# A fold without a product, one question at the end, and a start in another order: four small edits to an attention and experts kernel

## The chip, the cores and the metric

One core of a Trainium2 chip runs the kernel. The metric is device microseconds (us) of one execution; lower is better. The engines are TensorE (PE in the profile, its weight loads PEld), VectorE (DVE), ScalarE (ACT), GpSimd (POOL) and SyncE (SP), which issues most transfers. Each takes its own list of instructions in order and waits on semaphores for the others.

## The reference

Attention in which a query sees only the keys of its own cluster, and behind it a layer of experts in which each row goes to one expert of eight:

```python
# q, k, v: (4, 8, 768, 64); centroids: (8, 16, 64)
q_assign = argmax(normalized(q) @ normalized(centroids).T)   # 16 clusters per head; k_assign likewise
mask = q_assign[..., :, None] == k_assign[..., None, :]
scores = where(mask, q @ k.T / sqrt(64), -1e9)
x = softmax(scores) @ v            # heads side by side: (3072, 512)
logits = x @ w_gate                # 8 experts
e = argmax(logits);  gate = softmax(logits)[e]
y[rows of e] = relu(x[rows of e] @ w1[e]) @ w2[e]      # w1: 512 x 1024, w2: 1024 x 512
out = gate[:, None] * y
```

## The kernel before

Two heads make a pair, and there are 16 pairs (4 batches, 4 pairs each). The attention part is a list of jobs at numbered steps. A step makes three scores (`score`), then its jobs of part 0, then the three products with v of the step before (`attend`), then its jobs of part 1. For a pair, `turn` transposes q and k, `similar` and `similar2` make the similarities with the centroids and turn them, `assign` and `assign2` find the one-hots of the clusters, and `put` transposes those into `ohT`, which the scores add as a mask.

The start, before the first score:

```python
make_identity(nc, ident)
nc.vector.tensor_copy(ident_b, ident)
...   # norms of the centroids: three ScalarE functions, then seven VectorE steps
cps = ps_m.tile([P, 512], F32, name="mps")
nc.tensor.transpose(cps[:, 0:P], cn.rearrange("p a d -> p (a d)"), ident)
...
def turn(g, piece):
    ps = ps_s.tile([P, 2, 512], F32, name="sps").rearrange("p a c -> p (a c)")
    for i in range(4 if piece else 8):
        nc.tensor.transpose(ps[:, i * P : (i + 1) * P], ...q or k of the pair..., ident)
    flat = qk[g].rearrange("p w s -> p (w s)")
    if piece == 0:
        nc.vector.tensor_scalar_mul(flat[:, 0:S], ps[:, 0:S], D**-0.5)
        nc.scalar.copy(flat[:, S:1024], ps[:, S:1024])
    else:
        nc.scalar.copy(flat[:, 1024 : 2 * S], ps[:, 0 : 2 * S - 1024])
...
for g in range(NG):
    n = g * TG                      # TG = 4 steps for a pair
    if g == 1:
        for f, a in ((turn, (g, 0)), (turn, (g, 1)), (similar, (g,)), (similar2, (g,))):
            at(-1 if f is similar2 else -2, 1, f, *a)
    else:
        at(n - 4, 0, turn, g, 0)
        at(n - 4, 1, turn, g, 1)
        at(n - 3, 0, similar, g)
        at(n - 3, 1, similar2, g)
    at(n - 2, 0, assign, g)
    at(n - 2, 0, assign2, g)
    at(n - 1, 0, put, g)
```

The experts' part works in groups: eight experts, with two or three blocks of 128 rows and one last block of 32 rows each, and two groups of a single block of 128 for what overflows. (Three blocks have been worked ahead, during and behind attention.) For each group, `layer1` makes the hidden rows, the next group's rows are transposed, and `layer2` makes the sums. The 32 rows would use a quarter of PE's columns; so four products of two hidden blocks each stand side by side in the four quarters of an accumulator, and their four partial sums have to be added across quarters. Before, that was a product with `fold`, four 32x32 identities on top of each other:

```python
def wide():                                   # three of these, in turn
    return ps_s.tile([P, 2, 512], F32, name="sps")

def rows_out(g, j, m, zp):
    zo = p1.tile([P, Dm], F32, name="zo", bufs=3)
    nc.scalar.activation(zo[0:m], zp[0:m], AF.Copy, scale=...gate of the rows...)
    ins = nc.gpsimd.indirect_dma_start(out=out[:, :], ..., in_=zo[0:m], ...)     # scatter

def layer2(g):
    last = len(g["n"]) - 1
    zq = zc = None
    if g["n"][last] < P:
        zq = wide()
        n = FB * RQ // P                      # 2
        for i in range(n):
            for t in range(P // RQ):          # 4 quarters
                nc.tensor.matmul(zq[t * RQ : (t + 1) * RQ, 0, :],
                    lhsT=g["h"][:, t * n + i, last * P : last * P + RQ],
                    rhs=g["w"][1][:, t * n + i, :], start=(i == 0), stop=(i == n - 1))
        zc = p1.tile([P, Dm], F32, name="zo", bufs=3)
        nc.vector.tensor_copy(zc, zq[:, 0, :])
    for j, m in enumerate(g["n"]):
        if m < P:
            continue
        zp = wide()[:, 0, :]
        for fb in range(FB):                  # 8
            nc.tensor.matmul(zp, lhsT=g["h"][:, fb, j * P : (j + 1) * P], rhs=g["w"][1][:, fb, :], ...)
        rows_out(g, j, P, zp)
    if zc is not None:
        zf = wide()[0:RQ, 0, :]
        nc.tensor.matmul(zf, lhsT=fold, rhs=zc, start=True, stop=True)
        rows_out(g, last, RQ, zf)
```

At the end two numbers, found on the chip, are asked for by every engine: whether more overflow groups are needed than two, and whether the inputs call for a general path. Neither is so for these inputs, and both bodies are jumped over:

```python
nx = nc.values_load(xe[0:1, NX : NX + 1], min_val=0, max_val=NX)
general = nc.values_load(xe[0:1, NX + 1 : NX + 2], min_val=0, max_val=1)
with tc.If(nx > XU):
    ...   # more groups, in a loop
...
with tc.If(general > 0):
    in_general(...)
```

## Time and profile before

| | |
|---|---|
| time, median of 3 runs | 864.28 us (863.96 to 864.37) |
| span of the profiled execution | 862.4 us |
| PE busy | 832.5 us, 97% |
| DVE, ACT, POOL busy | 307.7, 271.2, 107.4 us |
| mean granted PE clock | 0.993 |

The page of the profile divides the span into 40 slices of 21.6 us. A digit is the busy share of an engine in a slice in tenths (9 is 90% or more), and in the row PEclk it is the granted clock of PE in tenths of full speed. A line of a group or of the timeline has the source line (L345), the engine, the operation, what is written and read, the form of the tiles and a count; an fp32 product shows as two records. In square brackets stands how long the engine had been idle and what ended the wait. The chain of waits follows the work that ended last back to the start, and "issue" in it is time for which the profile shows no cause. Sequencer steps (register loads, branches, semaphores, drains) aren't counted as busy; the trace keeps a record of each.

Attention takes the first 430 us or so, the experts the rest.

### The profile page before, as it was taken

Reading aid. Unit: us, or ns where it says so; the run is one execution under the profiler, and the core shown is the slowest. Engines: PE = TensorE matmul, PEld = TensorE weight load, DVE = VectorE, ACT = ScalarE, POOL = GpSimd, SP = SyncE. Lnnn points to the kernel's source line nnn. Section 1 sums busy time; section 2 is a strip of 40 time slices with the busy share of each in tenths; the row PEclk is TensorE's granted clock in tenths of the full one; section 3 lists DMA queues with packets and bytes.
Section 4 is the critical chain, followed back from the end, with each engine's and each line's share of the span. In section 5 each row is a group of like instructions: output and inputs, shape, how many; then the busy total and the mean of one; then the engine's idle time right before and its main releaser. Section 6 shows DMA issues by size and latency. Waiting matters only on the chain.

```text
span 862.4 us, 10765 instructions
## 1 busy us (share of the span) xinstructions
PE 832.5 (97%) x4397; PEld 435.3 (50%) x4397; DVE 307.7 (36%) x543; ACT 271.2 (31%) x422; POOL 107.4 (12%) x165
## 2 busy tenths in 40 slices
PE   4999999999999999999999999999999999999994
PEld 3444544444445444444576646645444454545472
DVE  2655566565565665875543101010101010101000
ACT  3554544554545555544311111111111111110010
POOL 3000000000000000130004211302020303010010
PEclk8999999999999999999999999999999999999998
DMA  9025320482222122210060245434242423312010
GB/s 203 1 57 217 88 55 11 121 251 56 55 81 59 46 55 56 93 38 1 8 274 15 66 141 205 159 110 152 110 150 110 164 98 119 136 67 90 24 38 7
DMA packets 76186, 81.69 MB, mean 95 GB/s; under 512 B 52831, under 2 KB 56927, under 8 KB 75616
## 3 DMA queue, kind: packets, MB, share of 16 engines
q1 hardware_dynamic: 70208, 60.82, 23.0%
q0 software_dynamic: 5248, 20.04, 6.5%
q8 instruction: 37, 0.61, 0.3%
q14 instruction: 21, 0.17, 0.1%
q10 hardware_dynamic: 672, 0.05, 0.1%
HBM read 68.26 MB, written 13.68 MB: 95 GB/s over the span
## 4 chain that ended last, share of the span: by engine, by line
PE 46%; issue 38%; POOL 8%; DVE 5%; ACT 1%; DMA 0%; POOLq 0%; ACTq 0%; DVEq 0%
PE sps L673 14%; PE O L693 14%; PE mps L711 4%; PE sps L676 3%; POOL out_dram L316 3%; POOL xg L270 3%; PE sps L599 3%; PE sps L301 2%; PE mps L613 2%; DVE T L685 2%; PE sps L754 2%; PE sps L651 1%; POOL oh_c L468 1%; PE mps L624 1%; PE sps L345 1%
## 5 line engine op out<-in xcount | busy, mean ns | idle before, releaser
L678 ACT ACTIVATE A<-sps 128x768 f32<-128x768 f32 x192 | 154.4, 810 | 71.1 <-PE sps L676 70.0
L301 PE MATMUL sps<-xgT,w 128*128 128x416 f32 (+2 forms) x640 | 175.2, 434 | 1.1 <-ACT xgT L290 1.1
L673 PE MATMUL sps<-qk 64*128 64x384 f32 x768 | 163.7, 501 | 0.5 <-DVE x L757 0.5
L345 PE MATMUL sps<-w,h_sb 128*128 128x512 f32 x368 | 160.6, 595 | 1.3 <-DVE h_sb L309 0.9
L301 PEld LDWEIGHTS sps<-xgT,w 128*128 128x128 f32 x640 | 111.1, 190 | 67.5 <-issue 49.8
L685 DVE TENSOR_TENSOR T<-T,A 128x768 f32<-128x768 f32 x128 | 122.6, 958 | 47.6 <-ACT A L678 37.6
L693 PE MATMUL O<-A,v_in 128*64 128x384 f32 x768 | 138.0, 494 | 0.0
L309 DVE TENSOR_SCALAR h_sb<-sps 128x416 f32<-128x416 f32 (+2 forms) x34 | 18.7, 550 | 316.6 <-PE sps L301 316.6
L345 PEld LDWEIGHTS sps<-w,h_sb 128*128 128x128 f32 x368 | 69.1, 190 | 91.7 <-issue 85.6
L673 PEld LDWEIGHTS sps<-qk 64*128 64x128 f32 x768 | 68.1, 187 | 36.5 <-issue 33.7
L693 PEld LDWEIGHTS O<-A,v_in 128*64 128x64 f32 x768 | 49.4, 136 | 69.7 <-issue 68.2
L315 ACT ACTIVATE zo<-sps,xg 128x512 f32<-128x512 f32 (+1 forms) x34 | 23.3, 685 | 180.0 <-PE sps L345 171.0
L316 POOL DMA_INDIRECT out_dram<-zo,s_idx x34 | 33.0, 970 | 319.0 <-ACT zo L315 316.1
L676 PE MATMUL sps<-ohT 64*128 64x384 bf16 x384 | 66.2, 324 | 2.2 <-DVE ohT L656 2.2
L311 ACT ACTIVATE h_sb<-sps 128x416 f32<-128x416 f32 (+2 forms) x34 | 16.5, 484 | 162.8 <-DVE h_sb L309 162.8
L681 DVE SCALAR_TENSOR_TENSOR T<-A 128x768 f32<-128x768 f32 x32 | 30.7, 959 | 82.1 <-ACT A L678 82.1
L634 POOL TENSOR_TENSOR sim<-sim,first_c 128x384 f32<-128x384 f32 x16 | 16.0, 997 | 291.3 <-DVE sim L633 291.3
L270 POOL DMA_INDIRECT xg<-x_rows,g_idx x34 | 33.3, 980 | 22.8 <-issue 9.8
L676 PEld LDWEIGHTS <-ohT 64*128 64x128 bf16 x384 | 22.1, 94 | 26.5 <-DVE ohT L656 5.4
L701 ACT COPY xT<-O 128x384 f32<-128x384 f32 x32 | 15.4, 481 | 31.4 <-PE O L693 31.4
L711 PE MATMUL mps<-T,one_row 128*32 128x384 f32 x128 | 23.7, 492 | 0.0
L345 PE MATMUL sps<-w,h 128*128 128x512 f32 x48 | 21.3, 597 | 1.4 <-ACT h L311 1.4
(191 smaller groups left out, 532.2 us busy)
## 6 DMA issues: line engine op xcount, KB each, us to landing
w<-in_moe_w_dram SPq DMA_DIRECT2D x20, 2048.0 KB, 8.7
x_rows<-x POOLq DMA_DIRECT2D x4, 1548.0 KB, 7.2
q_in<-in_q_dram SPq DMA_DIRECT2D x32, 192.0 KB, 4.5
k_in<-in_k_dram SPq DMA_DIRECT2D x32, 192.0 KB, 4.6
v_in<-in_v_dram SPq DMA_DIRECT2D x16, 384.0 KB, 3.4
xg<-x_rows,g_idx POOLq DMA_INDIRECT x34, 5.1
out_dram<-zo,s_idx POOLq DMA_INDIRECT x34, 2.9
csb<-in_centroids_dram ACTq DMA_DIRECT2D x1, 32.0 KB, 1.8
```

What stands on the lines that cost most here:

```text
L270: nc.gpsimd.indirect_dma_start(out=g["xg"][0:m, j, :], out_offset=None, in_=x_d[0 : g["rows"], :], in_offset=bass.IndirectOffsetOnAxis(ap= ...
L301: nc.tensor.matmul(o, lhsT=g["w"][0][:, c, fb * P : (fb + 1) * P], rhs=g["xT"][:, c, :cols], start=(c == 0), stop=(c == DB - 1),)
L316: ins = nc.gpsimd.indirect_dma_start(out=out[:, :], out_offset=bass.IndirectOffsetOnAxis(ap=g["si"](j)[0:m], axis=0), in_=zo[0:m], in_offs ...
L345: nc.tensor.matmul(zp, lhsT=g["h"][:, fb, j * P : (j + 1) * P], rhs=g["w"][1][:, fb, :], start=(fb == 0), stop=(fb == FB - 1),)
L599: nc.tensor.transpose(ps[:, i * P : (i + 1) * P], rows[g, "qk"[w]][:, j].rearrange("p a d -> p (a d)"), ident)
L673: nc.tensor.matmul(ps[:, a, 0:HS], lhsT=qk[g][r, 1, ks], rhs=qk[g][r, 0, qs], start=True, stop=False)
L676: nc.tensor.matmul(ps[:, a, 0:HS], lhsT=ohT[g][r, 1, ks], rhs=ohT[g][r, 0, qs], start=False, stop=True)
L678: nc.scalar.activation(A[u], ps[:, :, 0:HS], AF.Exp)
L681: nc.vector.scalar_tensor_tensor(T[g, half], in0=A[u - 1], scalar=1e-9 / P, in1=A[u], op0=ALU.add, op1=ALU.add)
L685: nc.vector.tensor_tensor(T[g, half], T[g, half], A[u], op=ALU.add)
L693: nc.tensor.matmul(O[g, half][a * D : (a + 1) * D, 0:HS], lhsT=rows[g, "v"][:, a, j, :], rhs=a_[:, a, :], start=(j == 0), stop=(j == NQ - 1),)
L711: nc.tensor.matmul(ps[half * 32 : (half + 1) * 32, 0:HS], lhsT=one_row[:, i, :] if i < 2 else wg[:, g % HP, :], rhs=t[half][:, i, :] if i ...
```

## The change

It has four parts.

- The four partial sums of the 32 rows are added by ScalarE copies and VectorE adds beside the products of the full blocks, rather than by a product with `fold` behind them. `fold` and what fills it go.
- The two questions become one: a third number says whether either of them is to be asked, and the two stand inside that branch. It costs one more small VectorE instruction. The tiles of the extra groups come from pools of their own, opened inside the branch.
- The second pair's `similar` comes behind the first pair's `put`, and its `similar2` behind the first three scores. ScalarE scales the second pair's queries, so that VectorE, which is at the first one-hots then, needn't.
- Twelve products of the identity with itself, whose result nobody reads, stand at the start, to keep PE busy before there is anything to do.

```diff
     def layer2(g):
         last = len(g["n"]) - 1
-        zq = zc = None
         if g["n"][last] < P:
-            zq = wide()
+            zq = wide()[:, 0, :]
             ...                        # the same eight products
-            zc = p1.tile([P, Dm], F32, name="zo", bufs=3)
-            nc.vector.tensor_copy(zc, zq[:, 0, :])
+            zc = pools["wk"].tile([RQ, P // RQ, Dm], F32, name="zc", bufs=1)
+            for t in range(1, P // RQ):
+                nc.scalar.copy(zc[:, t, :], zq[t * RQ : (t + 1) * RQ, :])
+            nc.vector.tensor_tensor(zc[:, 0, :], zc[:, 1, :], zq[0:RQ, :], op=ALU.add)
+            for t in range(2, P // RQ):
+                nc.vector.tensor_tensor(zc[:, 0, :], zc[:, 0, :], zc[:, t, :], op=ALU.add)
+            rows_out(g, last, RQ, zc[:, 0, :])
         for j, m in enumerate(g["n"]):
             ...                        # the full blocks, as before
-        if zc is not None:
-            zf = wide()[0:RQ, 0, :]
-            nc.tensor.matmul(zf, lhsT=fold, rhs=zc, start=True, stop=True)
-            rows_out(g, last, RQ, zf)
...
-        for t in range(P // RQ):
-            nc.gpsimd.tensor_copy(fold[t * RQ : (t + 1) * RQ, :], ident[t * RQ : (t + 1) * RQ, t * RQ : (t + 1) * RQ])
...
         make_identity(nc, ident)
         nc.vector.tensor_copy(ident_b, ident)
+        ps = ps_m.tile([P, 512], F32, name="mps")
+        for i in range(12):
+            nc.tensor.matmul(ps[:, 0:P], lhsT=ident, rhs=ident, start=True, stop=True)
...
             if piece == 0:
-                nc.vector.tensor_scalar_mul(flat[:, 0:S], ps[:, 0:S], D**-0.5)
+                if g == 1:
+                    nc.scalar.mul(flat[:, 0:S], ps[:, 0:S], D**-0.5)
+                else:
+                    nc.vector.tensor_scalar_mul(flat[:, 0:S], ps[:, 0:S], D**-0.5)
...
             if g == 1:
-                for f, a in ((turn, (g, 0)), (turn, (g, 1)), (similar, (g,)), (similar2, (g,))):
-                    at(-1 if f is similar2 else -2, 1, f, *a)
+                at(-2, 1, turn, g, 0)
+                at(-2, 1, turn, g, 1)
+                at(-1, 1, similar, g)
+                at(0, 0, similar2, g)
...
         nc.vector.tensor_tensor(xe_f[:, NX : NX + 1], ove[0:1, E - 1 :], bad[0:1, 3:4], op=ALU.mult)
+        nc.vector.scalar_tensor_tensor(
+            xe_f[:, NX + 2 :], in0=xe_f[:, NX : NX + 1], scalar=XU + 0.5, in1=xe_f[:, NX + 1 : NX + 2],
+            op0=ALU.is_ge, op1=ALU.add,
+        )
         nc.vector.tensor_copy(xe, xe_f)
...
-    nx = nc.values_load(xe[0:1, NX : NX + 1], min_val=0, max_val=NX)
-    general = nc.values_load(xe[0:1, NX + 1 : NX + 2], min_val=0, max_val=1)
-    with tc.If(nx > XU):
-        ...
     mctx.close()
     late.close()
-    with tc.If(general > 0):
-        in_general(...)
+    more = nc.values_load(xe[0:1, NX + 2 : NX + 3], min_val=0, max_val=2)
+    with tc.If(more > 0):
+        nx = nc.values_load(xe[0:1, NX : NX + 1], min_val=0, max_val=NX)
+        general = nc.values_load(xe[0:1, NX + 1 : NX + 2], min_val=0, max_val=1)
+        with tc.If(nx > XU):
+            ...                        # the same loop, with pools of its own
+        with tc.If(general > 0):
+            in_general(...)
```

## The prediction

> **What bounds the kernel now.** I read the page first, then the chain of waits and the timeline of the first 30 us and of the last 75, and then the granted clock by stretches.

> ```profile
> PE 832.5 (97%) x4397; PEld 435.3 (50%) x4397; DVE 307.7 (36%) x543; ACT 271.2 (31%) x422; POOL 107.4 (12%) x165
> PE   4999999999999999999999999999999999999994
> PEclk8999999999999999999999999999999999999998
> ```

> TensorE (PE) has no free slice but the first and the last: 29.9 us of 862.4 are idle. So work taken off PE comes out of the time, work added to other engines costs nothing unless PE waits for it, and idle time can be won only in the first and the last 20 us. The change works in all three places.

> Place one, the chain of waits from 14 to 24 us (start, length, what):

> ```profile
> 15.53 0.56 DVE top L640
> 16.09 0.02 issue
> 16.12 0.56 DVE oh L641
> 16.68 0.88 DVE qk L603
> 17.56 0.14 issue
> 17.69 2.29 PE mps L613 x8
> 19.98 1.39 PE sps L651 x12
> 21.38 0.64 PE mps L624 x3
> 22.02 1.58 PE sps L673 x4
> 23.60 0.28 PE sps L676 x2
> ```

> The first pair's one-hots are ready at 16.68. Their transposes (L651) start at 19.9, because VectorE first scales the second pair's queries (L603) and PE, in program order, first makes that pair's similarities (L613). The first score is whole at 23.88, and PE has been full since. The clock over the same time (length, busy us and count per engine, then granted clock):

> ```profile
> 13.47:16.88 3.41, 0.57 (x6) 0.33 (x3) 2.23 (x5) 0.00 (x0) 2.19 (x10) 1.00 1.15 254
> 16.88:20.29 3.41, 2.60 (x12) 0.78 (x13) 0.66 (x1) 1.06 (x3) 2.78 (x19) 0.50 1.11 201
> 20.29:23.71 3.42, 3.42 (x20) 2.25 (x19) 0.56 (x1) 1.46 (x3) 0.01 (x1) 0.50 0.00 0
> ```

> PE stands idle from 14.04 to 17.69, and from 16.88 to 23.71 it has half its clock, just where the chain runs through it. The trace's matmul records show it half before 10.05 too: transposes start 0.213 us apart until then and 0.109 after.

> Place two, the fold of the 32-row sums, in the timeline of an expert's end:

> ```profile
> 513.72 1.04 PE L352 MATMUL sps<-zo,fold 128*32 128x512 f32 x2
> 513.87 0.69 ACT L315 ACTIVATE zo<-sps,xg 128x512 f32<-128x512 f32 x1 [6.10 <-PE sps L345]
> 514.69 2.48 PEld L301 LDWEIGHTS sps<-xgT,w 128*128 128x128 f32 x11 [0.84 <-ACT zo L315]
> ```

> The product sits between the expert's last second-layer matmul and the next expert's first. In the records 1.498 us lie between the starts of those two, at each of the eight experts; where no fold lies between, as at 835.66 to 836.09, it is 0.43.

> Place three, the end. The last rows are scaled at 851.47 (0.69), their scatter issued at 852.43 (0.98). The records of GpSimd's sequencer then have a semaphore step for the scatters from 853.02 to 854.66 (the scatter's last byte lands at 854.39), the second question's register load at 854.69 (0.31), its branch at 855.06, and a drain from 855.53 to 861.56. The others are done at 855.75.

> [...] L603 of the second pair had its input at 14.04 and ran at 16.59, behind the one-hots. [...] Here the second question's branch keeps PE 3.34 us and ScalarE 1.83, with instruction packets of 16384 and 8192 bytes at 853.09.

> **The change part by part.**

> *Fold.* Removed: 8 products. Each saves 1.498 - 0.43 = 1.07 us of PE; 8 x 1.05 to 1.07 = 8.4 to 8.5. Added per expert: three ScalarE copies of 32x512 (a 128x512 copy from PSUM takes 0.586, a 32-row activation 0.677 against 0.687 for 128 rows, so rows don't count: 3 x 0.6 to 0.7 = 1.9), three VectorE adds [...], and the scaling, 0.68, which was there before. That is 4.7 us of a chain beside 14 to 21 us of second-layer products; ScalarE idles 8.56 there before the first zo. The accumulator of the partial sums is held some 2.6 us and wanted again 14 us later (third full block, or the next expert's first hidden block). One VectorE copy (0.69) goes. On the path: nothing. Sum -8.4.

> *Start.* 12 idle products are 24 records; at 0.213 cold they fill 1.45 (identity ready at 1.35) to about 6.6, just before cn's transpose at 6.66, which VectorE and ScalarE set. So PE is at full clock from about 6.6 instead of 10.05. The first eight transposes then end at 7.8, not 8.83, and the whole chain up to the one-hots moves by 1.0: ready at 15.66. The put follows at once, at 15.7, and needs 0.84 (what L651 takes warm, at 38.15): 16.55. Copy to ohT 0.80, VectorE's half 0.56: ready at 18.0. Meanwhile PE makes the second pair's similarities, 0.8 warm (75.5 to 76.3), to 17.3, and the first half of the score, 0.65, to 18.0. L676 ends at about 18.5: 5.4 earlier than 23.88. Owed afterwards: the three transposes of similar2, 0.36 warm. That leaves 5.0. The second pair's scale on ScalarE takes some 0.8 while it waits for PE anyhow. Its data are there: the last k of that pair lands at about 10.5, its transposes move to 11.5. The second assign keeps its place, so the wait of 0.82 at 38.15 stays.

> *End.* One question instead of two takes GpSimd's second load and branch off: 855.53 - 854.69 = 0.8, if the drain is as long after that. PE's and ScalarE's far branches now follow the first question, PE's beside its last products; neither was last. I count 0.5.

> *Rest.* One VectorE instruction more (0.15) ahead of xe, for which the first gathers wait (472.42): at most 0.2. Four copies of 32x32 on GpSimd go, off the path.

> All as hoped: 8.4 + 5.0 + 0.8 = 14.2, 850.1 us.

> **The rivals.** (a) *The clock falls again.* PE would idle from 12.85 to 15.7, 2.9 us instead of 3.65. The window 13.47 to 16.88 would hold 1.2 us of work (34%) instead of 17%. For: 17% was enough to fall, and where the limit lies this trace can't say. Against: twice the work, and a shorter gap. If it falls at 16.88, 3.4 to 6.8 us run at half clock and cost 1.7 to 3.4: the start gains 1.6 to 3.3, time 852 to 853.5. I give it a third. (b) *The drain is tied to the scatter, not to what is before it.* For: it lasts 6.03 us, far longer than anything it visibly waits for. Then the end gains nothing: 850.9. Half. (c) *The idle products run into the path.* Cold at 0.22 or more a record they end at 6.7 to 6.9 and delay cn's transpose by up to 0.3. (d) *The new copies hold PE up*: ScalarE's queue now has them between relu and zo, and a hidden block that waits for ScalarE would cost up to 1 us an expert and eat the whole fold. Against: every wait of PE for ScalarE is there already short (0.84 at the fold, hidden by it), and zo's first use is 7 us after the copies. 5%; time 858.

> **Range and chances.** 14.2, less 0.8 for (a) (a third of 2.5), 0.4 for (b), 0.2 for (c) and the rest, is 12.8 to 13.4: 850.9 predicted. The low end, 849.2, is 0.9 below the hoped-for sum, for terms of that size that I don't see; the worst that I count (a with b, and some of d) 854. 2% is 17.3 us; all three parts at their best don't reach it, so faster by over 2% has 4%, and nothing seen makes it slower than before by 2%.

> **What would show it.** Fold: the first layer's first matmul starts 0.43 after the last of the second layer, no wait on zc. Start: idle products from about 1.45 to 6.6, transposes 0.109 apart from the first, the put within 0.1 of the one-hots at about 15.7, first score whole at 18.5, clock 1.00 throughout. End: a drain near 6.0 us, and 0.8 less between the last scatter and the end. The prediction is wrong if PE's busy time falls but gaps appear between experts, or if the clock is 0.50 after 16.9.

## The result, and the profile after

The changed kernel takes 851.27 us (median of four runs, 849.61 to 851.56), beside 864.12 for the kernel before, timed with it: 0.9847 of its time, with a 95% interval of 0.983 to 0.9864. That is 12.9 us less. 13.4 were forecast (850.9, with a range of 849.2 to 854).

From the page of the changed kernel, the busy times and two rows of the 40 slices:

```profile
PE 825.9 (97%) x4405; PEld 437.9 (52%) x4405; DVE 317.6 (37%) x559; ACT 286.1 (34%) x447; POOL 106.7 (13%) x161
PE   7999999999999999999999999999999999999994
PEclk9999999999999999999999999999999999999998
```

PE is still full in all slices but the first and the last; its first slice went from 4 to 7, mostly with products that nobody reads. DVE and ACT got 10 and 15 us more to do. The span of the profiled execution fell from 862.4 to 849.3 us. PE is full in between, so the 13.08 us can be assigned by the starts of the same matmuls in the records of both traces:

| stretch | how it is read | us less |
|---|---|---|
| start | first product with v starts at 24.83, before at 27.85 | 3.01 |
| eight folds | 1.069 at the changeover of each expert, and 0.104 just behind it | 9.39 |
| two overflow groups | two gaps before their first products are shorter by 0.07 each | 0.15 |
| end | start of the last second-layer matmul to the end of the span, 11.61 before and 11.08 after | 0.53 |
| sum | | 13.08 |

In the experts' part no other step between the starts of matmuls differs by more than 0.03 us.

**The fold.** The timeline of the changed kernel at an expert's end (start, length, engine, line, what; L352 is the second layer, L303 the next expert's first layer):

```profile
509.75 0.19 PEld L352 LDWEIGHTS sps<-w,h_sb 128*128 128x128 f32 x1 [0.24 <-issue]
510.18 0.19 PEld L303 LDWEIGHTS sps<-xgT,w 128*128 128x128 f32 x1 [0.24 <-issue]
510.61 1.62 PE L303 MATMUL sps<-xgT,w 128*128 128x288 f32 x6
```

The weight loads go on every 0.43 us across the changeover as they do inside a layer. In the matmul records the step from the last L352 to the first L303 is 0.429 us at all eight experts; it was 1.498. The step after it is shorter too, by 0.104 at each of the eight (0.350 for 0.453 at five of them, where the first layer works on more rows), which wasn't in the forecast. The added work, by groups with their shapes kept apart (count, then busy us and mean ns, then idle time before and what ended it):

```profile
L342 ACT COPY zc<-sps 32x512 f32<-32x512 f32 x24 | 13.9, 578 | 8.3 <-PE sps L335 8.1
L345 DVE TENSOR_TENSOR zc<-zc 32x512 f32<-32x512 f32 x16 | 10.9, 679 | 0.6
L343 DVE TENSOR_TENSOR zc<-zc,sps 32x512 f32<-32x512 f32 x8 | 5.4, 675 | 24.7 <-ACT zc L342 24.7
L317 ACT ACTIVATE zo<-zc,xg 32x512 f32<-32x512 f32 x8 | 5.8, 720 | 17.6 <-issue 11.1 <-DVE zc L345 6.5
```

Per expert that is 3 x 0.578 + 0.675 + 2 x 0.679 + 0.720 = 4.49 us of chain, where 4.7 were estimated; the part of the adds in that was the author's estimate, which no trace had shown. Nothing on PE waits for it: PE's waits for ScalarE in this part are what they were (1.4 us in sum before second-layer products and 1.1 before one of the first layer, in both kernels).

**The start.** The chain of waits from the first pair's one-hots to the first whole score (start, length, what):

```profile
15.32 0.57 DVE oh L647
15.89 0.05 issue
15.94 0.84 PE sps L657 x12
16.78 1.44 PE mps L619 x8
18.22 1.58 PE sps L679 x4
19.80 0.32 PE sps L682 x2
```

The put (L657) is 0.05 us behind the one-hots, where it was 3.3 us behind before, and takes the 0.84 that was worked out for it. But L619, the second pair's similarities, takes 1.44 us and not 0.8, and the first half of the score 1.58 and not 0.65. The stretches of the granted clock say why (length; busy us and count of PE, PEld, DVE, ACT and POOL; clock; DMA share; GB/s):

```profile
13.30:16.71 3.41, 0.77 (x12) 0.67 (x12) 1.43 (x3) 1.10 (x3) 2.63 (x15) 1.00 1.27 256
16.71:20.13 3.42, 3.42 (x18) 1.40 (x18) 0.56 (x1) 1.28 (x2) 1.53 (x10) 0.50 1.30 216
```

PE worked 0.77 us (23%) of the first stretch, and in the next one it had half its clock, from 16.71 to 20.13. This is rival (a), and one of the two signs by which the prediction said that it would be wrong ("if the clock is 0.50 after 16.9"). The first score is whole at 20.12, not 18.5. The idle products themselves, in the timeline of the start:

```profile
1.41 5.34 PE L547 MATMUL mps<-ident 128*128 128x128 f32 x24 [1.41 <-POOL ident masks.py:199]
6.82 0.33 PE L583 MATMUL mps<-ident,cn 128*128 128x128 f32 x1
```

They end at 6.75 and push cn's transpose (cn is what the centroids become once they are scaled) from 6.66 to 6.82, which is rival (c), 0.16 us. The clock rose at 6.47.

**The end.** These are the records of GpSimd's sequencer, in us from the start of the last scatter's issue (852.43 before, 839.88 after):

| | before | after |
|---|---|---|
| first branch, then the next record | 0.34, 0.52 | 0.34, 0.83 |
| semaphore step for the scatters | 0.59 to 2.23 | 0.98 to 2.60 |
| second question's load and branch | 2.26 and 2.63 | none |
| last byte of the scatter lands | 1.96 | 2.35 |
| drain | 3.10 to 9.13 | 2.64 to 8.59 |

Before, the drain began 0.87 us behind the semaphore step, with the second load and branch between; now it follows at once, after 0.04. But the semaphore step, as long as before (1.64 and 1.63), begins 0.39 later. The jump over both bodies takes 0.49 us from the branch to the next record, about as the second question's did (0.47, 855.06 to 855.53), and it now stands ahead of that step, where the first question's jump over its own body took 0.18. One more semaphore record, 0.08, stands there too. The drain lasts 5.95 us and not 6.03. In sum 9.13 - 8.59 = 0.54, which is the 0.53 of the table.

### The profile page after: what moved, and what is told of

The parts are those of the page before. It is cut to its first block, busy times and chain, and to the rows that moved or that the text cites. A ratio compares the mean times of both kernels' runs of the same rounds, so it can differ in the third digit from the quotient of the medians.

```text
span 849.3 us, 10793 instructions
## 1 busy us (share of the span) xinstructions
PE 825.9 (97%) x4405; PEld 437.9 (52%) x4405; DVE 317.6 (37%) x559; ACT 286.1 (34%) x447; POOL 106.7 (13%) x161
## 4 chain that ended last, share of the span: by engine, by line
PE 47%; issue 38%; POOL 8%; DVE 5%; ACT 1%; POOLq 0%; DVEq 0%; ACTq 0%
PE sps L679 15%; PE O L699 14%; PE mps L717 4%; PE sps L682 3%; POOL out_dram L318 3%; POOL xg L272 3%; PE sps L602 3%; PE sps L303 2%; DVE T L691 2%; PE mps L619 2%; PE sps L760 2%; PE sps L657 1%; POOL oh_c L467 1%; PE mps L630 1%; PE sps L352 1%
## 5 line engine op out<-in xcount | busy, mean ns | idle before, releaser
L303 PE MATMUL sps<-xgT,w 128*128 128x416 f32 (+2 forms) x640 | 174.3, 433 | 1.1 <-ACT xgT L292 1.1
L352 PE MATMUL sps<-w,h_sb 128*128 128x512 f32 x368 | 160.6, 595 | 1.2 <-DVE h_sb L311 0.8
L303 PEld LDWEIGHTS sps<-xgT,w 128*128 128x128 f32 x640 | 111.8, 190 | 64.6 <-issue 53.6
L352 PEld LDWEIGHTS sps<-w,h_sb 128*128 128x128 f32 x368 | 69.1, 190 | 91.5 <-issue 85.5
L317 ACT ACTIVATE zo<-sps,xg 128x512 f32<-128x512 f32 x26 | 17.9, 687 | 132.6 <-PE sps L352 123.5
L640 POOL TENSOR_TENSOR sim<-sim,first_c 128x384 f32<-128x384 f32 x16 | 16.0, 999 | 289.3 <-DVE sim L639 289.3
L352 PE MATMUL sps<-w,h 128*128 128x512 f32 x48 | 21.3, 596 | 1.4 <-ACT h L313 1.4
```

Source lines behind the costliest of these rows:

```text
L303: nc.tensor.matmul(o, lhsT=g["w"][0][:, c, fb * P : (fb + 1) * P], rhs=g["xT"][:, c, :cols], start=(c == 0), stop=(c == DB - 1),)
```

## The experiments

Each was timed beside the kernel before and is compared with it. "Theory A" and so on are alternatives named in what was expected.

### Each part alone

**1. The fold alone**, with the rest as before:

```diff
-            zc = p1.tile([P, Dm], F32, name="zo", bufs=3)
-            nc.vector.tensor_copy(zc, zq[:, 0, :])
+            ...                        # three copies, three adds, scaling: as in the change
-        if zc is not None:
-            ...                        # the product with fold
```

> The kernel before with nothing changed but the fold (copies and adds for the product). In the profile after, the next expert's first matmul starts 0.43 us after the last one of the second layer instead of 1.50, and the first layer's second matmul follows 0.35 behind the first instead of 0.45. Theory A (each fold costs its two records and two changes of the weights' form, and one late weight load behind it, 1.07 + 0.10): 8 x 1.17 = 9.4 us, 854.7. Theory B (only the 1.07 of the prediction's sum is won, the 0.10 belongs to something else that came in with the change): 8.6 us, 855.5. Theory C (the copies and adds take something back): less than 8.

Measured: 854.66 us (853.72 to 854.74), ratio 0.9886 (0.987 to 0.9901), 9.7 us less than the 864.34 of the kernel before beside it. In its trace the changeover step is 0.429 and the one behind it 0.350, as in the changed kernel. The fold is worth 9.4 and not 8.4, as theory A had it, and it brings this without the other parts. By the records the eight changeovers bring 9.37 here.

**2. The order alone**, `similar` behind `put`, `similar2` behind the first scores, the scale on ScalarE:

```diff
-                for f, a in ((turn, (g, 0)), (turn, (g, 1)), (similar, (g,)), (similar2, (g,))):
-                    at(-1 if f is similar2 else -2, 1, f, *a)
+                at(-2, 1, turn, g, 0)
+                at(-2, 1, turn, g, 1)
+                at(-1, 1, similar, g)
+                at(0, 0, similar2, g)
```

> The kernel before with only the second pair's similarities moved behind the first put, and its scale on ScalarE; no idle products. Theory A (order and clock both matter): the one-hots come at 16.68 as before, the put at 16.75, partly at half clock because PE idles 2.7 us ahead of it; first score whole at about 21.3 instead of 23.9, less 0.4 owed: 2 us won, 862. Theory B (the gain of the start is all order, the idle products do nothing): the whole 3.0 us, 861.1.

Measured: 862.22 us (861.42 to 863.15), ratio 0.9976 (0.9967 to 0.9986), 2.1 us less, which is theory A's time. Its stretches, in the same columns as above:

```profile
12.79:16.21 3.42, 1.88 (x17) 1.62 (x15) 1.11 (x2) 2.31 (x5) 0.49 (x1) 1.00 1.30 235
16.21:19.62 3.41, 1.66 (x22) 0.94 (x23) 1.11 (x2) 0.99 (x2) 2.89 (x18) 1.00 1.28 250
```

But theory A's way there (a put at 16.75, partly at half clock) is not what this execution shows. The stretch before these, from 9.38, is 91% busy, and the clock rose at its end, 12.79; behind the one before that (5.97 to 9.38), 63% busy, it did not. In the kernel before the stretches fell otherwise, and the clock rose at 10.05. So here the first pair's work comes later, the gap before the put, which starts at 17.96, lies in two stretches that are 55% and 49% busy, and the clock stayed at 1.00 through both. Five of the ten runs have this one's mean clock (0.996) and take 861.4 to 862.0 us; the other five have 0.994 or 0.995 and take 862.4 to 863.2, and no profile tells what the clock did in them.

**3. The idle products alone:**

```diff
+        ps = ps_m.tile([P, 512], F32, name="mps")
+        for i in range(12):
+            nc.tensor.matmul(ps[:, 0:P], lhsT=ident, rhs=ident, start=True, stop=True)
```

> The kernel before with only the twelve idle products added. Theory A (they bring the first transposes to full clock, and the clock falls again in the gap before the put, as before): the one-hots come 0.8 us earlier, 863.3. Theory B (they keep the clock up to the first score as well): the second pair's similarities, the put and the first score also run warm, 2.5 us or more, 861.5.

Measured: 862.93 us (861.64 to 863.65), ratio 0.9985 (0.9979 to 0.9992), 1.4 us less. That lies between the two theories, nearer A. Its stretches:

```profile
13.77:17.18 3.41, 0.14 (x2) 0.17 (x4) 1.98 (x3) 0.25 (x1) 2.92 (x14) 1.00 1.16 260
17.18:20.59 3.41, 3.41 (x21) 1.52 (x19) 0.00 (x0) 1.09 (x3) 2.08 (x14) 0.50 0.99 178
```

In the old order the gap is longer (4% busy), and the clock falls at 17.18. It is back at 20.59, after one stretch and not two as in the kernel before, and that one was full from end to end (3.41 us of PE), while the first of the two before was 76% busy (2.60).

**4. One question for two**, the rest as before:

```diff
-    with tc.If(nx > XU):
-        ...
-    with tc.If(general > 0):
-        in_general(...)
+    more = nc.values_load(xe[0:1, NX + 2 : NX + 3], min_val=0, max_val=2)
+    with tc.If(more > 0):
+        ...                            # both questions inside
```

> The kernel before with only the one question. Theory A (GpSimd's drain of about 6 us starts when its questions are done and is as long as ever): 0.6 us, 863.5. Theory B (the drain ends a fixed time after the last scatter has landed): no change.

Measured: 863.75 us (862.96 to 864.08), ratio 0.9993 (0.9985 to 1.0001), 0.6 us less. The interval touches 1, so the time alone doesn't prove it. The trace agrees with it: the drain starts 2.64 us after the last scatter's issue began, as in the changed kernel, and not 3.10, and lasts 5.95; from the start of the last second-layer matmul to the end of the span it is 11.08 us for 11.61.

The four medians add up to 9.7 + 2.1 + 1.4 + 0.6 = 13.8; together they gave 12.9. The difference of 0.9 is less than the 1.95 over which the changed kernel's runs spread, so it alone proves no overlap; but if there is one, the start is the place to look.

### The clock at the start

**5. The changed kernel with eleven more idle products** in the gap, behind the second pair's transposes:

```diff
+        def idle(n):
+            ps = ps_s.tile([P, 2, 512], F32, name="sps")
+            for i in range(n):
+                nc.tensor.matmul(ps[:, 0, 0:P], lhsT=ident, rhs=ident, start=True, stop=True)
...
                 at(-2, 1, turn, g, 1)
+                at(-2, 1, idle, 11)
```

> The changed kernel with eleven more idle products behind the second pair's transposes, in PE's gap before the first put (some 2.4 us at full clock, the gap has 2.9). Theory A (in the changed kernel the clock falls because that gap leaves a window of 3.4 us too empty, and costs some 1.7 us): the clock stays at 1.00 from its first rise to the end, the first score is whole at about 18.3 instead of 20.1, median 849.6, and the executions lie closer together. Theory B (what is won there is lost again, because PE is not what the first 30 us wait for): the clock stays up and the time is within 0.5 us of 851.3. Theory C (the idle products run late and delay the put): above 851.5.

Measured: 849.64 us (849.57 to 849.73), ratio 0.9832 (0.9818 to 0.9845). Stretches and then the chain of waits of this kernel:

```profile
13.48:16.89 3.41, 3.16 (x37) 2.87 (x39) 1.34 (x3) 1.01 (x3) 2.72 (x16) 1.00 1.26 257
16.89:20.31 3.42, 3.42 (x27) 1.36 (x28) 0.56 (x1) 2.85 (x4) 1.44 (x10) 1.00 1.25 210
```

```profile
16.03 0.84 PE sps L657 x12
16.87 0.78 PE mps L619 x8
17.65 0.84 PE sps L679 x4
18.50 0.19 PE sps L682 x2
```

The gap is filled (93%), the clock holds, L619 takes 0.78 for 1.44, and the first score is whole at 18.69, beside the 18.5 of the forecast. The first product with v starts at 23.34, 1.49 us earlier than in the changed kernel; the spans differ by 1.5. What rival (a) took is this, and of the versions that still handle every input it is the best that was run. Its runs lie within 0.16 us, those of the changed kernel within 1.95.

**6. The changed kernel without its twelve idle products:**

```diff
-        ps = ps_m.tile([P, 512], F32, name="mps")
-        for i in range(12):
-            nc.tensor.matmul(ps[:, 0:P], lhsT=ident, rhs=ident, start=True, stop=True)
```

> The changed kernel without the twelve idle products. Theory A (the parts add, as their single runs do: -9.7, -2.1, -1.4, -0.6): 1.4 us more than the changed kernel, 852.7. Theory B (with the order changed, the idle products bring less, since the parts sum to 13.8 and the whole change won 13.1): 0.5 to 0.8 more, 852.

Measured: 851.85 us (851.4 to 852.15), ratio 0.9857 (0.9842 to 0.9872). This is 0.6 above the changed kernel and within its spread, so the idle products bring little there. The stretches of the profiled execution:

```profile
13.00:16.41 3.41, 3.31 (x15) 3.06 (x15) 1.11 (x2) 1.19 (x3) 0.62 (x1) 1.00 1.31 243
16.41:19.82 3.41, 1.95 (x23) 1.08 (x24) 1.20 (x3) 1.75 (x5) 2.86 (x20) 1.00 1.03 232
```

(The clock column has 1.00 in the first stretch because the trace records no change before 16.41. The transposes, 0.213 us apart until then, say that the clock was half.) Cold transposes put the one-hots later, so the put starts at 18.02. But the cold work also fills PE up to the gap, the clock comes at 16.41 and isn't lost again, though the next stretch, with the gap in it, is only 57% busy. Two delays stand against each other: a cold beginning with a warm score here, where the put is 2.1 us later (18.02 for 15.94), and a warm beginning with a cold score in the changed kernel, where it takes 1.5 longer from the put to the first whole score (4.18 for 2.66). So the twelve products alone are worth 0.6 in this order, and the twelve and the eleven of experiment 5 together 851.85 - 849.64 = 2.2 us. The eleven without the twelve were not run. That the clock comes as late as 16.41 may be chance, too: the two stretches ahead of the first one shown, from 6.17 and from 9.58, are 77% and 78% busy, and it did not rise behind them; with other edges it rose at 10.05 behind one of 91% (the kernel before).

**10. Experiment 5 with ten products at the beginning for twelve:**

```diff
-        for i in range(12):
+        for i in range(10):
```

> The kernel with the eleven more idle products, with ten instead of twelve at the start. Theory A (twelve run 0.16 us into the path: the centroids' transpose started at 6.82 in the changed kernel and 6.66 before): 0.15 us less, 849.5. Theory B (ten leave a gap ahead of that transpose in which the first full-clock window can fail[...]): in some executions the clock comes later and the median is 850 or more, with a wider spread.

Measured: 850.04 us (850.01 to 852.88), ratio 0.984 (0.9827 to 0.9853). The intervals of this and of experiment 5 overlap, but its runs scatter: three at 850.0, one at 851.0, which is the profiled one, and one at 852.9. The stretches of the profiled run:

```profile
3.41:6.83 3.42, 2.64 (x13) 2.34 (x11) 1.69 (x8) 2.92 (x4) 1.99 (x6) 1.00 1.36 224
6.83:10.24 3.41, 3.03 (x15) 2.69 (x16) 1.40 (x3) 0.14 (x1) 0.09 (x1) 1.00 1.35 224
```

(Here too the 1.00 is for want of a record; the transposes are 0.213 us apart up to the last of them at 9.51.) The first stretch has a hole where the ten products had ended and cn wasn't ready. It is 77% busy, and the clock came only at the end of the next, 89% busy one. So the put starts at 17.0 for 16.03. The three runs at 850.0 are no worse than experiment 5, since the kernel before took 864.70 beside this one and 864.32 beside that; the other two are what theory B expected. In the profiled run the two products fewer went with a first rise at 10.24, where experiment 5 had it at 6.65.

**9. Experiment 5 with the scale of the second pair back on VectorE:**

```diff
-                if g == 1:
-                    nc.scalar.mul(flat[:, 0:S], ps[:, 0:S], D**-0.5)
-                else:
-                    nc.vector.tensor_scalar_mul(flat[:, 0:S], ps[:, 0:S], D**-0.5)
+                nc.vector.tensor_scalar_mul(flat[:, 0:S], ps[:, 0:S], D**-0.5)
```

> The kernel with the eleven more idle products, with the second pair's scale back on VectorE; the order of the change stays. Theory A (in order, the scale waits behind the first one-hots on VectorE; ScalarE's two copies of that pair wait for it, and ScalarE's copy to ohT behind them): the put starts at 16.0 as before, ohT is ready at 19.3 instead of 18.0, first score whole at about 19.9, 1.2 us more than with ScalarE, 850.8. Theory B (the order alone is enough, the scale finds room): 849.6.

Measured: 851.21 us (850.99 to 852.75), ratio 0.9851 (0.9836 to 0.9866). Lines of its timeline:

```profile
15.91 0.95 DVE L606 TENSOR_SCALAR qk<-sps 128x768 f32<-128x768 f32 x1
16.90 0.37 ACT L607 COPY qk<-sps 128x256 f32<-128x256 f32 x1 [4.34 <-DVE qk L606]
17.01 1.64 PE L616 MATMUL mps<-qk,cblk 128*32 128x384 f32 x8
17.17 0.59 ACT L609 COPY qk<-sps 128x512 f32<-128x512 f32 x1
17.81 0.14 PEld L616 LDWEIGHTS mps<-qk,cblk 128*32 128x32 f32 x4 [0.66 <-ACT qk L609]
17.64 0.82 ACT L658 COPY ohT<-sps 128x768 bf16<-128x768 bf16 x1
18.49 0.56 DVE L659 TENSOR_SCALAR ohT<-sps 128x768 bf16<-128x768 bf16 x1 [1.63 <-ACT ohT L658]
```

The put comes at the same time (16.05), but L606 runs behind the one-hots, ScalarE's two copies of that pair (L607, L609) wait for it (4.34 us), and PE's similarities of the second pair (L616) wait for the copies: the weights of their second half are loaded at 17.81, right behind L609, and the eight records take 1.64 us for 0.78 in experiment 5. The score comes behind them in PE's order. ScalarE's copy of the put into ohT stands behind the two copies too, but VectorE has the rest of ohT ready at 19.05, before the first half of the score ends at 19.50. The first score is whole 0.97 us later (19.70 for 18.73 at the ScalarE instruction that reads it). The times differ by 1.57; about 0.4 of it lies between the two timings, since the kernel before took 864.70 beside this one and 864.32 beside experiment 5. So one 0.95 us instruction on the wrong queue would undo about 1 us of the new order.

### The fold and the end, measured by themselves

**8. The kernel before with its product with fold made twice:**

```diff
             nc.tensor.matmul(zf, lhsT=fold, rhs=zc, start=True, stop=True)
+            nc.tensor.matmul(zf, lhsT=fold, rhs=zc, start=True, stop=True)
```

> The kernel before with each fold's product made twice, the second over the first: eight products more and no change of the weights' form more. Theory A (a fold of 1.17 us is 0.91 of product, two records 0.454 apart, and 0.26 for the changes between forms around it): 8 x 0.91 = 7.3 us, 871.6. Theory B (each product costs the whole 1.17 wherever it stands): 9.4 us, 873.7.

Measured: 870.65 us (870.59 to 871.59), ratio 1.008 (1.0066 to 1.0093), 6.3 us more. A changeover in its timeline:

```profile
631.34 1.05 PE L352 MATMUL sps<-zo,fold 128*32 128x512 f32 x2
632.22 1.02 PE L353 MATMUL sps<-zo,fold 128*32 128x512 f32 x2
633.17 0.30 PEld L301 LDWEIGHTS sps<-xgT,w 128*128 128x128 f32 x2 [0.84 <-issue]
633.17 1.31 PE L301 MATMUL sps<-xgT,w 128*128 128x416 f32 x3
```

A second product costs 0.86 us by the records (two of 0.43), 8 x 0.86 = 6.9; both theories had it too high. From the first product with v to the last second-layer matmul the trace has just these 6.87 us more (829.82 for 822.95). The time has 6.3, as the profiled execution's start came 0.67 earlier (27.18 for 27.85); nothing of the program differs there, but the edges of the clock's stretches do, and the full clock was back at 20.89 for 23.71. One product with its changeovers cost 1.17. The other 0.31 is the change of form, weights of 32 columns between weights of 128: the step into fold's product is 0.523 rather than 0.429, the one between its two records 0.453, the one out of it 0.523 again, where the load of the next weights begins late (the 0.84 idle on PEld), and the step behind is 0.104 longer (0.094 + 0.024 + 0.094 + 0.104 = 0.316). This part was paid once for the two products together. The same steps of 0.523 and then 0.104 more (0.533) stand in both kernels where the eight quarter products, whose weights have 32 columns too, end and the full blocks begin; so here it went with the form and not with `fold`.

**7. The changed kernel without the question and both bodies behind it.** It leaves out what handles other inputs; for these it computes the same.

```diff
-    more = nc.values_load(xe[0:1, NX + 2 : NX + 3], min_val=0, max_val=2)
-    with tc.If(more > 0):
-        ...
```

> The changed kernel with no question at the end at all: it leaves out the branch with the extra groups and the general path, which these inputs don't enter. Theory A (GpSimd's drain has a length of its own, about 6.0 us, from when GpSimd gets there): without the wait for the scatters in the branch it starts right behind the last scatter's issue, 1.6 us earlier, and the end comes as much earlier, 849.7. Theory B (the drain ends some 6.2 us after the last scatter has landed, whatever stands between): the drain is longer by what it starts earlier, 851.0 to 851.3.

Measured: 848.74 us (848.38 to 850.01), ratio 0.9822 (0.9809 to 0.9835). That is 2.5 us less than the changed kernel's median, but the runs of both spread by more than 1.6. In the traces the part from the start of the last second-layer matmul to the end of the span is 9.41 us for 11.08, 1.67 less, where theory A had 1.6. In the sequencer's records the issue of the last scatter starts at 840.21 and ends at 841.20, its last byte lands at 842.18, and the drain ends at 847.15: 6.94 us after the start of the issue, for 8.59 with one question and 9.13 with two. (The drain's record itself begins at 839.97 here, ahead of the issue, and so lasts 7.18.) Its end is 5.95 after the issue's end and 4.97 after the landing, where it was 7.17 after the landing before the change and 6.24 behind it. So in these three kernels the drain's end came 5.95 to 6.03 us after GpSimd was done with what stands ahead of it, and not at a fixed time after the landing of the scatter. What the drain does in these 6 us isn't shown.

## Why the prediction came out right

*Fold, forecast 8.4, measured 9.4.* The mechanism was right: the product goes, and nothing waits for the adds. The term of 1.05 to 1.07 an expert was too small, since it counted only the step across the fold. The first layer's second matmul had also been late, by 0.104, behind a product of another form (experiment 8): 8 x 0.104 = 0.83 of the 1.0 missed, and the rest is 1.069 for the 1.05 of the sum; 1.173 x 8 = 9.39. Experiment 1 has the same, alone.

*Start, forecast 5.0 if warm, 3.0 measured.* This is the step that did not go as forecast: "clock 1.00 throughout" was given as its sign, and the clock was 0.50 for 3.41 us. The order did as was worked out: one-hots at 15.88 (15.66 forecast), put 0.05 behind, no wait of the score for VectorE or ScalarE. Rival (a), which got a third, is what happened: the gap's stretch was 23% busy, 34% was estimated. The stretch's edges fell 0.17 us earlier than assumed, so that only the put's first 0.77 us was in it. It cost 1.5 us (experiment 5), just under the 1.7 to 3.4 stated. A second term was too small: similar2's 0.36. It takes 0.48 where it now stands, and the score behind it resumes with 0.84 rather than 0.65 for its first half, 0.67 in all. And the first score itself, resuming behind the similarities, takes 0.84 for the 0.65 of its first half, so that even with the clock held it is whole at 18.69 and not 18.5. With the clock held, experiment 5 so gains 27.85 - 23.34 = 4.5 of the 5.0.

*End, forecast 0.8, counted 0.5, measured 0.53.* Rival (b), the drain tied to the scatter, is half right. The scatter's landing doesn't set it (7.17, 6.24 and 4.97 us from the landing to the drain's end with two, one and no questions), but the questions in front of it push it back, so it gains. The term of 0.8 was too large because the longer jump, now ahead of the semaphore step, pushes that step back by 0.39; the forecast had it free. The traces with one question (experiment 4 and the changed kernel) both have the drain at 2.64, those with two (the kernel before and experiment 1) at 3.10 and 3.09.

*Rest, at most 0.2 lost; nothing found.* The gaps before the two overflow groups are even 0.15 shorter in sum. *Rival (c)* took 0.16, less than the 0.3 allowed. *Rival (d)* is out: PE's waits for ScalarE in the experts are the same.

So the forecast was near for a reason that it half contained: a fold 1.0 better than worked out, and a start 2.0 worse, of which 0.8 was allowed for. That these nearly cancel is luck. (The allowances gave 12.8 to 13.4, and the point, 13.4, is the upper end; the 12.9 measured is at the lower.) That the single parts add up to more than the whole fits experiments 5 and 6, in which order and idle products meet in one gap, but isn't clear of the spread. Why the changed kernel's own runs lie 1.95 us apart isn't shown. Its run with the highest mean clock (0.996) is the shortest, 849.61, near experiment 5. The gap before its put is 2.70 us long, as long as in experiment 2, where an edge of the stretches split it and the clock held; so it may be that in some runs the stretches fall so here as well. No profile of such a run was taken.

## What to carry to other kernels

Before an engine is made ready earlier, see whether it then idles longer: here idle products at the start alone brought the clock up and a gap took it away again, and both fills together gave 2.2 us against 0.6. Without them the start differed with where the edges of the clock's stretches fell (the full clock came at 9.94 in experiment 1 and at 16.41 in experiment 6), so one profile of it is one case; look at the spread of several runs. A small product of another form between large ones cost 1.17 us, 0.31 more than its own 0.86 (experiment 8), so read the records of the step behind it as well. What was added on two idle engines, 4.5 us beside 14 us of products, was free, but a 0.95 us scale behind the one-hots on VectorE brought the first score 0.97 us later (experiment 9), so even that has to stand where nothing that the first score needs waits for it.

## What the runs showed of the hardware that was not expected

```profile
836.09:839.51 3.42, 1.25 (x3) 0.19 (x1) 0.00 (x0) 0.69 (x1) 0.99 (x1) 1.00 0.01 2
839.51:842.92 3.41, 0.00 (x0) 0.00 (x0) 0.00 (x0) 0.00 (x0) 0.00 (x0) 0.50 0.06 19
```

```profile
849.73:853.15 3.42, 1.65 (x4) 0.38 (x2) 0.00 (x0) 0.69 (x1) 0.72 (x1) 1.00 0.03 7
853.15:856.56 3.41, 0.00 (x0) 0.00 (x0) 0.00 (x0) 0.00 (x0) 0.26 (x1) 1.00 0.10 27
```

It fell behind 37% and held behind 48%. So the emptiest stretch that held it was 48% busy and the fullest that lost it 37%; the emptiest that brought it was 84% busy and the fullest that did not 78%. What lies between, no run tells. The edges of the stretches differed from profile to profile: with the same twelve products the first rise came anywhere from 6.47 (the changed kernel) to 7.00 (experiment 7), and in kernels without them from 9.94 (experiment 1) to 16.41 (experiment 6).

**GpSimd's drain at the end** lasted 6.03 us with two questions (the kernel before, where the last scatter had landed 1.1 us before it began) and 5.95 with one (the changed kernel, where that was 0.3, and experiment 4). Without a question (experiment 7) it ended 5.95 us after the end of the scatter's issue, with the landing 1.0 us behind that end.

**Fewer rows didn't make the copy cheaper here**, as the prediction had assumed. A 32x512 copy took ScalarE 0.578 us (L342 of the changed kernel) and a 128x512 one 0.586 (L290 of the kernel before). VectorE's 32x512 adds took 0.675 and 0.679 (L343 and L345 of the changed kernel); no add of 128x512 stands beside them.
